# Two per-token rows through DRAM on ScalarE's queue, and all corrections on VectorE

## The chip, the cores and the metric

One core of one Trainium2 chip. The metric is the device time of one launch in microseconds (us), as the median of several runs; the span that a profile shows is about 1.8 us shorter. The runs that are compared ran on the same chip.

Engine names in the profile: PE is the matrix engine, DVE is VectorE, ACT is ScalarE, POOL is GpSimd, SP is the engine that here only issues transfers. ACTq and SPq are the instruction queues of ScalarE and SP when they issue a transfer. The prediction calls the transfers that SP and ScalarE issue HWDGE transfers. BU, in it, is the half-transformed data, which goes through DRAM and comes back in another order (the regrouping).

## The reference

```python
def reference(A_x, A_w_r, A_w_i, B_x, B_w_gate, B_w_up, B_w_down):
    x  = A_x                                   # (1, 2048, 640) bf16
    xn = _layernorm(x, axis=-1)                # eps 1e-5, no scale and shift
    s  = irfft2(rfft2(xn) * (w_r + 1j * w_i))  # over both axes
    g  = _silu((_gelu(xn @ w_gate) * (xn @ w_up)) @ w_down)   # 640 -> 1536 -> 640
    return x + s * g
```

Only the layer norm in front of `w_gate` and `w_up` matters here. For the first 512 tokens and the first two tiles of hidden features the kernel does not wait for the normalised input: it multiplies the raw `x`, and mends the product afterwards. With mean m and r = 1/sigma of a token, (x - m) r W = (x W + (-m) colsum(W)) r. The tokens lie along the free dimension of the product, so -m and r are needed as rows that stand on all 128 partitions. These rows are the subject of the change.

## The kernel before

The kernel is recorded as a list of tasks (`add`), each with the engines that may run it, an assumed duration, a rank and its inputs. A small simulator (`Plan.run`) then decides, before compilation, in which order each engine gets its instructions. A task's `land` is an assumed landing time, in ns, of a transfer; it overrides the simulator's own estimate. On the chip each engine works strictly in that order, so an instruction that waits holds all those behind it.

```python
# r and -m of 4 x 128 tokens lie as columns in RM; PE turns them into 8 rows, VectorE copies
# them out of PSUM, they go to DRAM (D5, 4 KB) and come back broadcast to 128 partitions (RB, 512 KB)
t  = add(rows_pe, "PE", ...)
t  = add(lambda e: nc.vector.tensor_copy(out=..., in_=sr.tile[0:8, 0, 0:P]), "DVE", ...)
rs = dma(D5, lambda: rt.tile[0:8, :], (0, -5, 0), 4096, after=[t], use=[rt])          # on SP
rb_in = dma(RB..., D5.rearrange("k t -> (k t)").partition_broadcast(P), (0, -5, 1), 524288, after=[rs])
...
def gate_up(grp, t):
    ...   # the matmuls of one tile of w_gate into pg and of w_up into pu (two PSUM buffers each)
    if not early:
        a = add(act, "ACT", ...)      # ge = gelu(pg)             -> frees pg
        u_done[grp, t] = add(mul, "DVE", ...)   # uT = pu * ge    -> frees pu
        return
    for k, (w, ps) in enumerate(((Wg, pg), (Wu, pu))):       # the two early tiles
        ...   # copy the raw product out of PSUM (IU for gate, R for up)
        m = add(... nc.vector.scalar_tensor_tensor(out=ev, in0=RB[:, 1], scalar=WSUM, in1=ev,
                                                   op0=mult, op1=add), "DVE", ..., after=[out, rb_in, ...])
        normed.append(add(... (nc.gpsimd if e == "POOL" else nc.vector).tensor_tensor(ev * RB[:, 0]),
                          "POOL" if k else "DVE", ..., after=[m]))
    ...   # then gelu and uT as above
...
with tc.manual_schedule():
    for t in plan.run():
        t.emit(t.on)
```

Beside these, ScalarE casts the folded halves of the Fourier transform out of PSUM (`mc<-sp`). Each cast frees a buffer that PE's next transform matmuls (`sp<-mb,F1T`) need.

## Time and profile before

| | before |
|---|---|
| time, median (lowest to highest) | 202.86 us (202.78 to 203.01) |
| span of the profiled run | 201.1 us |
| PE busy | 195.2 us, 97% |
| PE idle between 10 and 197 us | one hole of 0.38 us |
| RB, from issue to landing | 22.20 to about 29.7 us |

The prediction shows the views of this profile. Its lines read: start in us, duration, engine, source line, operation, output<-inputs, partitions x elements and type, count; in brackets the engine's idle time just before, and what ended it. These lines from the timelines of VectorE, GpSimd and PE (one fence each) are not among them:

```profile
29.71 0.75 DVE L920 SCALAR_TENSOR_TENSOR IU<-RB,WSUM,IU 128x512 f32<-128x512 f32 x1 [1.12 <-DMA RB<-D]
...
32.84 1.38 DVE L920 SCALAR_TENSOR_TENSOR IU<-RB,WSUM,IU 128x512 f32<-128x512 f32 x1
```

```profile
32.40 1.27 POOL L922 TENSOR_TENSOR R<-R,RB 128x512 f32<-128x512 f32 x1 [1.26 <-DVE R L920]
```

```profile
37.49 0.97 PE L970 MATMUL pg<-Wd,uT 128*128 128x320 bf16 x6 [0.38 <-ACT ge L903]
```

The first correction waits 1.12 us for RB; a correction beside GpSimd's multiply takes 1.38 instead of 0.75 us; and PE's only hole after 5.3 us is 0.38 us long.

### The profile page before, as it was taken

The page shows a single profiled execution, that of the slowest core. Times are in us where ns is not written, and L with a number is a line of the kernel's source. Part 1 is how long each engine was busy: PE and PEld are TensorE (multiplying, and loading weights), DVE is VectorE, ACT ScalarE, POOL GpSimd, SP SyncE. Part 2 cuts the span into 40 slices and gives each one's busy share as a digit, 9 for nine tenths or more (in the row PEclk, how much of TensorE's full clock was granted, in tenths as well). Part 3 has the DMA queues.
Part 4 walks back from the last instruction along what each step waited for, and adds up shares of the span by engine and source line. Part 5 has one row for each costly group of instructions (what it writes and reads, how often), then busy time and mean ns, then how long its engine had stood idle before and what let it go on. Part 6 is the DMA issues. An engine that isn't in the chain of part 4 may idle for free.

```text
span 201.1 us, 4125 instructions
## 1 busy us (share of the span) xinstructions
PE 195.2 (97%) x1527; PEld 117.4 (58%) x1527; DVE 149.7 (74%) x320; ACT 127.2 (63%) x224; POOL 33.1 (16%) x73
## 2 busy tenths in 40 slices
PE   7999999999999999999999999999999999999992
PEld 2994444566544555677755555467765555457781
DVE  3789969999323249999998999933257788887774
ACT  3898997974632768778775766333466565766421
POOL 2412347596000000000000000000004122211210
PEclk9999999999999999999999999999999999999999
DMA  6999999569949677333244210117704332332432
GB/s 175 329 316 325 344 392 235 126 165 196 301 128 375 223 202 178 103 93 115 61 126 126 75 50 16 68 49 221 317 3 135 96 132 100 98 107 92 130 103 65
DMA packets 35894, 32.62 MB, mean 162 GB/s; under 512 B 10910, under 2 KB 32930, under 8 KB 35874
## 3 DMA queue, kind: packets, MB, share of 16 engines
q1 hardware_dynamic: 34434, 29.49, 49.1%
q0 software_dynamic: 1152, 2.66, 4.8%
q10 hardware_dynamic: 288, 0.20, 0.5%
q8 instruction: 12, 0.20, 0.4%
q14 instruction: 8, 0.07, 0.1%
HBM read 22.51 MB, written 9.19 MB: 158 GB/s over the span
## 4 chain that ended last, share of the span: by engine, by line
PE 79%; DMA 10%; SPq 4%; DVE 3%; issue 1%; ACT 1%; DVEq 0%
PE pg L886 19%; PE pu L886 19%; PE pg L970 13%; PE pu L970 12%; DMA X<-in_A_x_dram 6%; SPq L303 4%; DMA RB<-D 4%; PE sp L697 3%; PE sp L830 3%; PE sp L772 2%; PE sp L806 2%; PE sp L670 2%; PE sp L532 1%; PE sp L690 1%; PE sp L824 1%
## 5 line engine op out<-in xcount | busy, mean ns | idle before, releaser
L886 PE MATMUL pu<-xnT,Wu 128*128 128x512 bf16 (+1 forms) x245 | 57.6, 366 | 0.0
L886 PE MATMUL pg<-xnT,Wg 128*128 128x512 bf16 (+1 forms) x245 | 57.5, 366 | 0.0
L907 DVE TENSOR_TENSOR uT<-pu,ge 128x512 bf16<-128x512 f32 x46 | 31.7, 689 | 20.9 <-PE pu L886 18.4
L970 PEld LDWEIGHTS <-uT 128*128 128x128 bf16 x396 | 37.8, 98 | 14.1 <-issue 0.6
L903 ACT ACTIVATE ge<-pg 128x512 bf16<-128x512 f32 x46 | 27.4, 597 | 25.5 <-PE pg L886 25.0
L886 PEld LDWEIGHTS <-Wg 128*128 128x128 bf16 x285 | 25.2, 98 | 22.1
L886 PEld LDWEIGHTS <-Wu 128*128 128x128 bf16 x285 | 25.1, 98 | 21.8
L970 PE MATMUL pg<-Wd,uT 128*128 128x320 bf16 (+2 forms) x204 | 30.5, 293 | 0.4 <-ACT ge L903 0.4
L970 PE MATMUL pu<-Wd,uT 128*128 128x320 bf16 (+1 forms) x192 | 29.7, 297 | 0.0
L296 ACT CAST ma<-sp 128x644 bf16<-128x644 f32 (+1 forms) x32 | 23.4, 792 | 9.7 <-PE sp L830 7.9
L932 POOL COPY xr<-s 1x1 bf16<-1x1 bf16 x1 | 0.2, 182 | 101.8 <-DVE s L856 101.8
L933 POOL DMA_DIRECT2D xr<-in_A_x_dram x16 | 8.8, 552 | 32.3 <-DVE res L957 31.7
L296 ACT CAST IU<-sp 128x640 bf16<-128x640 f32 x16 | 10.9, 691 | 4.2 <-PE sp L772 4.1
L979 ACT ACTIVATE th<-pg 128x320 f32<-128x320 f32 (+2 forms) x17 | 7.3, 427 | 9.9 <-PE pg L970 8.9
L296 ACT CAST Vt<-sp 128x640 bf16<-128x640 f32 x16 | 10.8, 691 | 3.7 <-PE sp L806 3.7
L984 DVE SCALAR_TENSOR_TENSOR G<-th,pg 128x320 bf16<-128x320 f32 (+1 forms) x16 | 7.7, 479 | 7.1 <-ACT th L979 6.9
L979 ACT ACTIVATE th<-pu 128x320 f32<-128x320 f32 (+1 forms) x16 | 7.0, 438 | 9.2 <-PE pu L970 9.0
L984 DVE SCALAR_TENSOR_TENSOR G<-th,pu 128x320 bf16<-128x320 f32 (+1 forms) x16 | 7.7, 480 | 5.6 <-ACT th L979 5.3
L296 ACT CAST mc<-sp 128x640 bf16<-128x640 f32 x15 | 9.8, 694 | 2.3 <-PE sp L533 1.3
L433 POOL TENSOR_TENSOR RSTD<-MVA,mh 128x1 f32<-128x1 f32 x12 | 8.4, 697 | 4.5 <-DVE MVA L415 3.7
L848 DVE TENSOR_TENSOR mb<-ma 128x640 bf16<-128x640 bf16 x8 | 3.9, 493 | 6.9 <-ACT ma L296 6.9
L750 DVE TENSOR_TENSOR R<-Y 64x644 bf16<-64x644 bf16 x16 | 7.8, 490 | 0.4
(107 smaller groups left out, 252.9 us busy)
## 6 DMA issues: line engine op xcount, KB each, us to landing
BU<-D SPq DMA_DIRECT2D x8, 640.0 KB
D<-mc SPq DMA_DIRECT2D x8, 320.0 KB
D<-IU SPq DMA_DIRECT2D x8, 320.0 KB
xr<-in_A_x_dram POOLq DMA_DIRECT2D x16, 160.0 KB, 2.6
out_dram<-res SPq DMA_DIRECT2D x15, 160.0 KB
Wg<-in_B_w_gate_dram SPq DMA_DIRECT2D x6, 320.0 KB
Wu<-in_B_w_up_dram SPq DMA_DIRECT2D x6, 320.0 KB
Wd<-in_B_w_down_dram SPq DMA_DIRECT2D x6, 320.0 KB
```

The source lines that it names most:

```text
L296: return nc.scalar.copy(out=out, in_=in_) if e == "ACT" else nc.vector.tensor_copy(out=out, in_=in_)
L303: return add(lambda e: nc.sync.dma_start(out=out() if callable(out) else out, in_=in_() if callable(in_) else in_), "SP", (430, 430), rank ...
L433: nc.gpsimd.tensor_tensor(out=rstd, in0=var, in1=mh, op=ALU.pow)
L697: nc.tensor.matmul(into(q, ri), lhsT=sZ.tile[:, q, ri, :], rhs=FM[:, kinds[q][2] + (4 if ri and kind == 0 else 0), :], start=False, stop=T ...
L750: nc.vector.tensor_tensor(out=o, in0=Yf[:, ::-3, :], in1=Yf[:, 1:3, :], op=ALU.subtract)
L886: nc.tensor.matmul(ps.tile[:, lo:hi + more], lhsT=w[:, c, t * P:(t + 1) * P], rhs=XR[:, c, lo + (lo > 0):hi + 1 if lo or more else hi] if ...
L903: nc.scalar.activation(out=ge.tile, in_=pg.tile if src is None else src, func=ACT.Gelu_apprx_tanh)
L907: nc.vector.tensor_tensor(out=u.tile, in0=pu.tile if src is None else src, in1=ge.tile, op=ALU.mult)
L933: nc.gpsimd.dma_start(out=sx.tile, in_=xv[:, n1, :])
L970: nc.tensor.matmul(ps.tile[:, 0:hi - lo], lhsT=uT[grp, ks[i]].tile[:, j * P:(j + 1) * P], rhs=Wd[:, ks[i], lo:hi], start=(i == 0), stop=(i ...
L979: nc.scalar.activation(out=th.tile[:, 0:hi - lo], in_=ps.tile[:, 0:hi - lo], func=ACT.Tanh, scale=0.5)
L984: nc.vector.scalar_tensor_tensor(out=G2.tile[:, lo:hi], in0=th.tile[:, 0:hi - lo], scalar=1.0, in1=ps.tile[:, 0:hi - lo], op0=ALU.add, op1 ...
```

## The change

The intent: RB waits on SP behind several microseconds of weight loads. On ScalarE's queue it should come earlier. The planner is told so (17.0 and 20.8 us), and places the corrections earlier. With the second multiply on VectorE too, no engine stands in the other's way.

```diff
-    rs = dma(D5, lambda: rt.tile[0:8, :], (0, -5, 0), 4096, after=[t], use=[rt])
-    rb_in = dma(RB.rearrange("p k n t -> p (k n t)"), D5.rearrange("k t -> (k t)").partition_broadcast(P), (0, -5, 1), 524288, after=[rs])
+    rs = add(lambda e: nc.scalar.dma_start(out=D5, in_=rt.tile[0:8, :]), "ACT", (600, 600), (0, -5, 0), after=[t], use=[rt], size=4096, land=17000)
+    rb_in = add(lambda e: nc.scalar.dma_start(out=RB.rearrange("p k n t -> p (k n t)"), in_=D5.rearrange("k t -> (k t)").partition_broadcast(P)),
+                "ACT", (600, 600), (0, -5, 1), after=[rs], size=524288, land=20800)
...
-            normed.append(add(lambda e, ev=ev: (nc.gpsimd if e == "POOL" else nc.vector).tensor_tensor(out=four(ev), in0=four(ev), in1=RB[:, 0], op=ALU.mult), *(("POOL", (1700, 1800), (1, 8)) if k else ("DVE", c_dve(512, 1), (0, 100))), after=[m], use=[ev]))
+            normed.append(add(lambda e, ev=ev: nc.vector.tensor_tensor(out=four(ev), in0=four(ev), in1=RB[:, 0], op=ALU.mult), "DVE", c_dve(512, 1), (0, 100), after=[m], use=[ev]))
```

## The prediction

> **What bounds the kernel now.** I read the page first, then the chain of waits, then the timelines of PE, ScalarE and the DMA-issuing SP queue from 10 to 40 us. The page's busy times and the chain's summary:
>
> ```profile
> PE 195.2 (97%) x1527; PEld 117.4 (58%) x1527; DVE 149.7 (74%) x320; ACT 127.2 (63%) x224; POOL 33.1 (16%) x73
> PE 79%; DMA 10%; SPq 4%; DVE 3%; issue 1%; ACT 1%; DVEq 0%
> ```
>
> PE is busy 195.2 of 201.1 us at full clock. The 5.9 us left are 1.21 at the start, 0.41 at 5.3 us, about 3.9 after the last matmul, and one hole of 0.38 at 37.1 us. So no change to VectorE, GpSimd or a transfer can win more than about 0.4 us unless it removes matmuls, and this one removes none. PE has no spare time after 5.3 us in which to win back a stall: whatever stops PE lengthens the run one for one.
>
> The chain passes through the transfers that the change moves:
>
> ```profile
> 4.39 5.97 DMA X<-in_A_x_dram
> 10.38 1.03 SPq L303
> ...
> 15.54 6.09 DMA X<-in_A_x_dram
> 21.64 0.52 SPq L303
> 22.20 7.48 DMA RB<-D
> 29.74 0.64 issue
> 30.38 0.68 DVE uT L907
> ```
>
> The reader should see two things. The broadcast RB takes 7.48 us from its issue, yet what it makes wait is small: in the wait view VectorE's first correction waited 1.1 us for it, and PE lost only the 0.38 us hole. And an issue on SP is released by the completion of a load issued six microseconds before (4.39 + 5.97 releases 10.38; 15.54 + 6.09 releases 21.64). The compiled instruction list explains it: HWDGE transfers take eight completion semaphores in turn, and each waits until the earlier user of its semaphore, eight transfers back, has landed. The SP timeline gives the landings:
>
> ```profile
> 10.38 1.03 SPq L303 DMA_DIRECT2D Wu<-in_B_w_up_dram  x1
> 11.45 1.49 SPq L303 DMA_DIRECT2D X<-in_A_x_dram  x2
> 12.99 1.24 SPq L303 DMA_DIRECT2D Wg<-in_B_w_gate_dram  x1
> 14.27 1.22 SPq L303 DMA_DIRECT2D Wu<-in_B_w_up_dram  x1
> ...
> 18.07 0.69 SPq L303 DMA_DIRECT2D Wu<-in_B_w_up_dram  x1
> ...
> 19.97 0.41 SPq L303 DMA_DIRECT2D D<-mc  x1
> 20.76 1.40 SPq L303 DMA_DIRECT2D Wd<-in_B_w_down_dram  x2
> ```
>
> The Wu load issued at 14.27 is the earlier user for the Wd load that starts at 20.76 after a 0.4 us wait, so it landed at 20.74. Between it and the first X load of 11.45 (tile 10) lie one X tile and two weight loads, 0.82 MB; at the 318 GB/s that the DMA view shows for 16 to 18 us that is 2.6 us, so X tile 10 landed at about 18.1. The issue at 18.07, which needed that semaphore, started without a visible wait: 18.05 us.
>
> ScalarE and PE at the moment where the change inserts the first transfer:
>
> ```profile
> 13.24 0.74 ACT L418 ACTIVATE th<-X 128x640 bf16<-128x640 bf16 x1
> 14.10 0.83 ACT L421 ACTIVATE th<-X,NM 128x640 bf16<-128x640 bf16 x1
> 14.93 1.18 ACT L903 ACTIVATE ge<-pg 128x512 bf16<-128x512 f32 x2
> 16.00 1.28 ACT L296 CAST mc<-sp 128x640 bf16<-128x640 f32 x2
> ```
>
> ```profile
> 15.85 1.24 PE L886 MATMUL pu<-xnT,Wu 128*128 128x512 bf16 x5
> 16.93 1.24 PE L886 MATMUL pg<-xnT,Wg 128*128 128x512 bf16 x5
> 18.01 0.38 PE L532 MATMUL sp<-mb,F1T 128*128 128x512 bf16 x1
> ```
>
> PE starts the pg group of 16.93 in the buffer that the first GELU (14.93) has emptied, and the transform of 18.01 in the buffer that the first cast (16.00) has emptied. Those two ScalarE instructions have about 1.4 us of slack, not more.
>
> **What the Trainium skill says.** "DMA: Bandwidth & Descriptors", section "Anatomy of one DMA", says that a semaphore wait belongs to the issuing sequencer, ahead of dispatch, and not to the DMA engines. The SP queue above behaves so; here it means ScalarE itself stands still. The same page, "Issuing engines are not separate DMA queues": issuing from another engine saves only sequencer time, the 16 engines are shared; the trace has them full (over 300 GB/s from 5 to 30 us), so the move adds no bandwidth. The same page, "Queues, rings and completion order": a DMA engine takes turns between queue rows by packets, so RB on ScalarE's row need not stand behind SP's backlog. No line of this trace shows that yet. "SBUF — State Buffer" calls the port pair of VectorE and GpSimd an exclusive lock. The trace agrees in tendency: the VectorE correction at 32.84 takes 1.38 us beside GpSimd's 1.27 us multiply at 32.40, and 0.75 us elsewhere; the uT multiply at 36.01 takes 1.16 instead of 0.67.
>
> **The change part by part.**
>
> 1. GpSimd loses two multiplies (1.27 and 1.36 us); VectorE gains two of about 0.68 us, 0.60 apart in the timeline: +1.2 us. The two slowed instructions give back 0.63 + 0.49 = 1.1 us. Net about zero, and it lies beside PE.
>
> 2. The move to D5 leaves SP (0.35 us) for ScalarE. In the compiled order it stands right after the mean pass that ends at 14.1 us and before the first GELU, and it waits for two semaphores: VectorE's copy (done 13.6 us) and the completion semaphore last used by X tile 10, which lands at 18.05. So ScalarE stops from 14.1 to 18.05: 4.0 us. The scheduler believed D5 would have landed by 17.0, and knows nothing of the semaphore. Issue 0.45 us (the X issue on ScalarE took 0.43): first GELU at 18.5, done at 19.1.
>
> 3. PE wanted that buffer at 16.93 and gets it at about 19.15: stall 2.2 us. It then wants the buffer of the first cast at 20.25. ScalarE after the GELU: variance pass 0.83, second GELU 0.50, cast 0.60, done at 21.0: stall 0.75 us.
>
> 4. RB follows on ScalarE at 21.0. It waits for D5 (issued 18.5, an estimate of 2.5 us by the page's fixed 2 us and some load, 21.0) and for the semaphore of the Wu load (20.74). ScalarE loses 0 to 0.5 us and 0.45 for the issue; the second cast ends at about 22.4, PE wants it at 22.4: 0.2 us. Sum so far 3.15 us.
>
> 5. RB lands about 4 us later, near 25.3: 2 us fixed by the page, and 0.52 MB at between half and all of 380 GB/s, 1.4 to 2.8 us (estimate). The new order has VectorE reach the first correction after the third uT multiply, near 23.8, so it stands for 1.5 us. The next uT multiply comes three corrections later (3 x 0.64 + 0.6 = 2.5 us), at 27.8; PE wants its pu buffer at about 28.3. No stall, unless RB lands after 25.8; I count 0.2 us.
>
> 6. The hole at 37.1 us (GELU of the last gate tile late) should go, since in the new order that GELU ends before PE wants its buffer: -0.38 us.
>
> 7. Later, SP issues five loads of the first spectral weights before the regrouping BU instead of after it, about 1.5 to 2.5 us later relative to PE. The first quarter of BU landed near 63.7 (an issue that needs its semaphore starts at 63.74) and is used at 65.83, so 2.1 us of slack: 0 to 0.4 us lost, counted 0.2.
>
> Sum: 2.2 + 0.75 + 0.2 + 0.2 - 0.38 + 0.2 = +3.2 us. Everything else shifts along with PE. 202.9 + 3.2 = 206.1 us, +1.6%.
>
> **The rivals.** (a) The intended effect: D5 lands at 17, RB at 20.8, corrections done by 27, the hole gone, 202.5 us. For it: RB indeed waits behind 6 us of backlog now, and a queue of its own takes turns. Against it: the hidden semaphore waits, and that there are only 0.4 us to win. (b) VectorE becomes the bound: from 15 to 25 us it is busy 9.6 of 10 us, and it now must do the corrections there while waiting in order for RB. If RB lands near 27, the uT multiplies release pu late and PE loses another 1.5 us: 207.5 to 208. For it: the lag of step 5 leaves only 0.5 us. Against it: ScalarE's stop has slowed PE and so given VectorE room. (c) The late start of BU costs 2 us more (208), if the weight loads hold the queue longer; against it, PE's own delay carries the whole chain along.
>
> **Range and chances.** Steps 2 to 4 depend on one landing known to about 0.3 us, on the issue time (0.4 to 1.1 us on SP under load) and D5's latency: about 1 us either way. Steps 5 and 7 add only upwards, up to 2 us. Range 204.4 to 207.8. The line of 2% is at 206.9: slower 0.28, within 0.70, faster 0.02, as the ceiling of gain is 0.4 us.
>
> **What would show it.** In the changed trace: ScalarE idle for about 4 us before the D5 issue, which starts near 18.1; the first GELU on pg near 18.5; PE idle about 2 us before the pg group that starts at 16.93 now, then some 0.7 us before the third transform; RB issued near 21 and landed near 25; the hole near 37 us gone; PE's busy sum unchanged. I am wrong if the D5 issue starts near 14 (the semaphore wait does not bind), if PE shows no hole between 16 and 23 us, or if PE's larger holes come at 28 us (rival b) or near 69 us (rival c).

## The result, and the profile after

| | before | after |
|---|---|---|
| time, median (lowest to highest, runs) | 202.85 us (202.78 to 203.01, 6) | 208.84 us (208.54 to 208.98, 6) |
| ratio of the mean times, 95% interval | | 1.0293 (1.0279 to 1.0306) |
| span of the profiled run | 201.1 us | 206.8 us |
| PE busy | 195.2 us | 196.4 us |
| mean granted clock | 1.00 | 0.989 |

A ratio here is the mean time of one kernel's fast runs over that of the other's in the same rounds, so it is not quite the ratio of the medians. The result is slower by 2.9%, 6.0 us, above the predicted range (204.4 to 207.8).

ScalarE's timeline of the kernel after (source lines from the change on are one higher than before):

```profile
18.45 0.53 ACTq L567 DMA_DIRECT2D D<-th  x1
19.02 0.60 ACT L904 ACTIVATE ge<-pg 128x512 bf16<-128x512 f32 x1 [4.99 <-DMA X<-in_A_x_dram]
...
20.80 0.69 ACT L296 CAST mc<-sp 128x640 bf16<-128x640 f32 x1
23.22 0.35 ACTq L568 DMA_DIRECT2D RB<-D  x1
23.61 0.69 ACT L296 CAST mc<-sp 128x640 bf16<-128x640 f32 x1 [2.12 <-DMA D<-th]
```

ScalarE stood twice. The first stop ends with the landing of an X tile that the first transfer does not read: the semaphore that it takes over. The second one waits for D5 itself: issued at 18.45, landed by 23.22, 4.8 us later. The cast of 23.61, whose input was ready, stood behind it.

VectorE's timeline of the kernel after:

```profile
24.83 0.69 DVE L908 TENSOR_TENSOR uT<-pu,ge 128x512 bf16<-128x512 f32 x1 [1.14 <-ACT ge L904]
28.00 0.75 DVE L921 SCALAR_TENSOR_TENSOR IU<-RB,WSUM,IU 128x512 f32<-128x512 f32 x1 [2.48 <-DMA RB<-D]
28.67 0.74 DVE L921 SCALAR_TENSOR_TENSOR R<-RB,WSUM,R 128x512 f32<-128x512 f32 x1
29.33 0.68 DVE L923 TENSOR_TENSOR IU<-IU,RB 128x512 f32<-128x512 f32 x1
29.93 0.68 DVE L908 TENSOR_TENSOR uT<-pu,ge 128x512 bf16<-128x512 f32 x1
```

RB landed at 28.00, only 1.7 us before its time on SP, and VectorE stood 2.48 us for it. In the new order three corrections stand ahead of the uT multiply of 29.93.

PE's timeline of the kernel after:

```profile
19.67 1.24 PE L887 MATMUL pg<-xnT,Wg 128*128 128x512 bf16 x5 [2.61 <-ACT ge L904]
21.54 0.58 PE L532 MATMUL sp<-mb,F1T 128*128 128x512 bf16 x1 [0.64 <-ACT mc L296]
...
22.03 2.34 PE L887 MATMUL pu<-xnT,Wu 128*128 128x512 bf16 x5
24.35 0.58 PE L532 MATMUL sp<-mb,F1T 128*128 128x512 bf16 x1
...
30.67 1.24 PE L887 MATMUL pu<-xnT,Wu 128*128 128x512 bf16 x5 [0.28 <-DVE uT L908]
...
43.04 0.39 PE L532 MATMUL sp<-mb,F1T 128*128 128x512 bf16 x1 [0.25 <-DVE mb L519]
```

The holes sum to 3.78 us. There is also the pu group of 22.03, which took 2.34 us instead of 1.24. The table by stretches of the same run shows why; after the busy times of PE, PEld, DVE, ACT and POOL its last three columns are the granted clock, the share of the DMA engines and GB/s:

```profile
18.00:20.00 2.00, 0.33 (x2) 0.19 (x2) 0.35 (x1) 0.98 (x2) 0.00 (x0) 1.00 1.14 337
20.00:22.00 2.00, 1.36 (x7) 0.47 (x5) 1.93 (x6) 1.49 (x4) 1.17 (x3) 0.85 1.12 332
22.00:24.00 2.00, 2.00 (x7) 0.77 (x6) 1.69 (x5) 0.39 (x1) 0.20 (x1) 0.50 1.13 324
```

PE ran at half clock behind its hole. And the DMA engines were full, 324 to 337 GB/s, while D5 was on its way.

The same work on PE starts later than before by these amounts: the first pg group after the stop by 2.74 us (16.93 to 19.67), the next by 5.19 (19.64 to 24.83), and from there it is 5.53 at the regrouped transform (65.83 to 71.36) and at the end of the last matmul (197.17 to 202.70). So the whole loss arises between 17 and 31 us, and 5.2 of it by 24.8 us.

### The profile page after: what moved, and what is told of

Same layout as the page of the kernel before. It is cut to its first block, busy times and chain, and to the rows that moved or that the text cites. A ratio compares the mean times of both kernels' runs of the same rounds, so it can differ in the third digit from the quotient of the medians.

```text
span 206.8 us, 4110 instructions
## 1 busy us (share of the span) xinstructions
PE 196.4 (95%) x1509; PEld 117.8 (57%) x1527; DVE 149.0 (72%) x321; ACT 126.9 (61%) x225; POOL 31.1 (15%) x71
## 4 chain that ended last, share of the span: by engine, by line
PE 80%; DVE 6%; DMA 6%; SPq 2%; issue 2%; ACT 1%; ACTq 0%; DVEq 0%
PE pu L887 21%; PE pg L887 19%; PE pg L971 12%; PE pu L971 12%; DMA X<-in_A_x_dram 6%; PE sp L698 3%; PE sp L831 3%; PE sp L773 2%; DVE uT L908 2%; SPq L303 2%; PE sp L807 2%; PE sp L532 2%; PE sp L671 2%; PE sp L691 1%; PE sp L825 1%
## 5 line engine op out<-in xcount | busy, mean ns | idle before, releaser
L887 PE MATMUL pg<-xnT,Wg 128*128 128x512 bf16 (+1 forms) x235 | 56.5, 365 | 3.1 <-ACT ge L904 2.6
L887 PE MATMUL pu<-xnT,Wu 128*128 128x512 bf16 (+1 forms) x237 | 58.3, 371 | 0.8 <-DVE uT L908 0.3
L887 PEld LDWEIGHTS <-Wu 128*128 128x128 bf16 x285 | 25.3, 98 | 22.8 <-issue 1.8
L296 ACT CAST mc<-sp 128x640 bf16<-128x640 f32 x16 | 10.8, 702 | 3.7 <-DMA D<-th 2.1
L433 POOL TENSOR_TENSOR RSTD<-MVA,mh 128x1 f32<-128x1 f32 x12 | 9.5, 797 | 1.0 <-DVE MVA L415 0.2
L418 ACT ACTIVATE th<-X 128x640 bf16<-128x640 bf16 x11 | 8.1, 739 | 0.0
```

Source lines behind the costliest of these rows:

```text
L296: return nc.scalar.copy(out=out, in_=in_) if e == "ACT" else nc.vector.tensor_copy(out=out, in_=in_)
L418: nc.scalar.activation(out=place(junk, (D,)), in_=x, func=ACT.Copy, scale=-1.0 / D, accum_out=less)
L433: nc.gpsimd.tensor_tensor(out=rstd, in0=var, in1=mh, op=ALU.pow)
L887: nc.tensor.matmul(ps.tile[:, lo:hi + more], lhsT=w[:, c, t * P:(t + 1) * P], rhs=XR[:, c, lo + (lo > 0):hi + 1 if lo or more else hi] if ...
```

## The experiments

Sixteen kernels, all with correct results, each beside the kernel before on the same chip. That kernel took 202.81 to 202.96 us in the median each time, so times of different rounds can be compared to about 0.2 us. (Beside run 16 one execution of the kernel before took 1155 us; it was left out as slow.)

| run | what is different | median us | ratio to before |
|---|---|---|---|
| 1 | before, all corrections on VectorE | 203.2 | 1.0017 |
| 2 | after, GpSimd keeps its multiplies | 209.61 | 1.0334 |
| 3 | after, issue and landing times told | 206.67 | 1.0187 |
| 4 | D5 and RB on GpSimd's queue, landings half told | 205.63 | 1.0128 |
| 5 | after, landings told | 207.3 | 1.0243 |
| 6 | GpSimd's queue, landings told | 202.7 | 0.9994 |
| 7 | after, D5's semaphore free earlier | 209.23 | 1.0326 |
| 8 | after, D5's semaphore free later | 211.26 | 1.0428 |
| 9 | after, RB issue and corrections moved back by hand | 210.42 | 1.0362 |
| 10 | GpSimd's queue, landings as in after | 208.87 | 1.0299 |
| 11 | after, PE's hole filled | 208.8 | 1.0293 |
| 12 | after, corrections moved back by hand | 209.05 | 1.0306 |
| 13 | after, later landings told, same end | 207.52 | 1.0245 |
| 14 | 13 with the semaphore earlier | 205.83 | 1.0152 |
| 15 | 13 with the semaphore later | 210.41 | 1.0379 |
| 16 | 13 with PE's hole filled | 207.04 | 1.0203 |

My theory after the result: the semaphore stop of ScalarE, then D5's slow landing, cost the time. The rivals: VectorE, which waits in order for RB; the half clock; the corrections on VectorE themselves.

### Runs 1 and 2: the two parts of the change alone

Run 1 is the kernel before with only the last line of the diff; run 2 is the kernel after without it.

> Half of the change: all corrections on VectorE, both transfers still on the SP queue. My theory (the loss comes from ScalarE standing still for completion semaphores that other transfers used before): within 0.3% of before, 202.4 to 203.4 us, no PE hole over 0.5 us. Rival (VectorE, with 1.2 us more of work in its busiest stretch, became the bound): at least 204.5 us.

> The other half: both transfers on ScalarE's queue, GpSimd keeps its two multiplies. My theory: as slow as the changed kernel, 208.0 to 209.5 us, with ScalarE idle near 5 us before the first transfer's issue at about 18.4 us and the PE clock at half for about 3 us after the hole. Rival (VectorE's extra work): near 203 to 204 us.

Run 1: 203.2 us, ratio interval 0.9991 to 1.0043; its profile has one hole of 0.64 us, near 49.5 us, where at most 0.5 was expected. Run 2: 209.61 us (209.44 to 209.93). So the multiplies cost nothing where they are, and the whole loss is that of the queue; beside it the move of the multiplies even helps (208.84 against 209.61). PE's holes of run 2:

```profile
23.81 0.38 PE L532 MATMUL sp<-mb,F1T 128*128 128x512 bf16 x1 [0.70 <-ACT mc L296]
...
30.73 1.24 PE L887 MATMUL pu<-xnT,Wu 128*128 128x512 bf16 x5 [1.10 <-DVE uT L908]
```

One thing I had expected was missing: after a first hole of 2.51 us the clock stayed full here. In place of the half clock PE waited, for the cast behind D5 (0.70 us) and for the uT multiply behind RB (1.10 us). That was the first sign that several limits lie on top of each other.

### Runs 3 and 4: tell the planner, or take another queue

```diff
 # run 3
+        at = max(at, getattr(t, "not_before", 0))     # in the planner
-..., "ACT", (600, 600), (0, -5, 0), after=[t], use=[rt], size=4096, land=17000)
+..., "ACT", (600, 600), (0, -5, 0), after=[t], use=[rt], size=4096, land=23200);  rs.not_before = 18500
-                "ACT", (600, 600), (0, -5, 1), after=[rs], size=524288, land=20800)
+                "ACT", (600, 600), (0, -5, 1), after=[rs], size=524288, land=28000);  rb_in.not_before = 23300
 # run 4
-    rs = add(lambda e: nc.scalar.dma_start(...), "ACT", ..., land=17000)
+    rs = add(lambda e: nc.gpsimd.dma_start(...), "POOL", ..., land=18500)
-    rb_in = add(lambda e: nc.scalar.dma_start(...), "ACT", ..., land=20800)
+    rb_in = add(lambda e: nc.gpsimd.dma_start(...), "POOL", ..., land=24000)
```

> The changed kernel, with its scheduler told what the trace measured: first transfer not before 18.5 us and landing at 23.2, broadcast not before 23.3 and landing at 28.0. Both stay on ScalarE's queue, only later in its order, behind work that is ready. My theory: ScalarE no longer stands still (under 0.7 us before each issue), PE has no hole over 0.5 us, 202.5 to 203.6 us, although the broadcast lands as late as in the changed kernel, near 28 us. Rival (ScalarE's queue itself is slow or harmful, whenever it is used): stays above 206 us.

> The changed kernel with both transfers issued by GpSimd, whose transfers take their semaphores from a separate set that nothing else uses at this time. My theory: the first transfer is issued near 14.5 us at once, as no foreign landing has to be awaited; ScalarE and PE run as before, 202.5 to 204 us. GpSimd may stand a few us for the landing of the first transfer, which delays some 1/sigma results. Rival (the 16 engines are full and any early broadcast takes bandwidth that PE needs): PE holes waiting for weights, above 205 us.

Both missed: 206.67 and 205.63 us. In run 3 the later place in the list gave both transfers other semaphores. RB's was one that a Wd load had used, and ScalarE stood 3.65 us for that load:

```profile
26.41 0.60 ACT L907 ACTIVATE ge<-pg 128x512 bf16<-128x512 f32 x1 [3.65 <-DMA Wd<-in_B_w_down_dram]
```

That stop left PE a hole of only 0.35 us. PE's largest hole came later: RB landed at 32.36 us, VectorE stood 2.52 us for it, and PE behind VectorE:

```profile
35.03 2.29 PE L890 MATMUL pu<-xnT,Wu 128*128 128x512 bf16 x5 [2.25 <-DVE uT L911]
```

So an order told to the planner moves the semaphores too, and run 3 doesn't test its theory. In run 4 GpSimd, whose semaphores nobody had used, issued D5 at 14.04 at once, and ScalarE never stood. But D5 landed 5.9 us later and RB another 8.4 us later, and now VectorE stood (its timeline, then PE's):

```profile
28.41 0.75 DVE L921 SCALAR_TENSOR_TENSOR IU<-RB,WSUM,IU 128x512 f32<-128x512 f32 x1 [4.24 <-DMA RB<-D]
```

```profile
29.82 1.24 PE L887 MATMUL pu<-xnT,Wu 128*128 128x512 bf16 x5 [1.81 <-DVE uT L908]
```

RB, issued right behind D5, came at 28.0 us from ScalarE's queue and at 28.4 from GpSimd's. From here on I held two causes: ScalarE stands (for the semaphore, then for D5), and VectorE stands for RB, because the plan puts the corrections at a landing that the full DMA engines don't give.

### Runs 5 and 6: the landings told, on either queue

```diff
 # run 5: the kernel after, D5 and its semaphore stay where they are
-..., size=4096, land=17000)            +..., size=4096, land=23200)
-..., size=524288, land=20800)          +..., size=524288, land=28000)
 # run 6: run 4 with
-..., size=4096, land=18500)            +..., size=4096, land=20000)
-..., size=524288, land=24000)          +..., size=524288, land=28500)
```

> The changed kernel, but its scheduler is told when D5 and RB really land (23.2 and 28.0 us in place of 17.0 and 20.8). In the instruction list D5 keeps its place on ScalarE and keeps X tile 10's completion semaphore; the RB issue moves behind the casts, and VectorE's corrections move behind the uT multiplies. Theory of two causes (ScalarE stands for the semaphore; VectorE stands in order for RB): the first stays whole, ScalarE idle from 14 to about 18.4 us and PE's hole of about 2.6 us near 17 to 19.7, the second goes (VectorE waits under 0.5 us for RB, no PE hole from uT near 30 us): 205.2 to 206.2 us. Rival, that the semaphore stop explains all 6 us of loss: 208.3 to 209. Rival, that the wait for RB explains all: under 204.

> The fourth experiment's kernel (D5 and RB issued by GpSimd, whose semaphores nobody else has used yet), but its scheduler is told the landings that that run showed (20.0 and 28.5 us). Theory of two causes: both are gone now, ScalarE and PE run as in the kernel before and VectorE waits for RB under 0.5 us; 202.4 to 203.6 us, PE holes under 0.8 us in sum between 10 and 45 us. Rival, that the corrections on VectorE or the transfers on another queue cost something of their own that these two do not cover: 204.5 us or more, with a PE hole near 30 to 42 us that a uT multiply ends.

Run 6 hit: 202.7 us, interval of the ratio 0.9978 to 1.0009, and PE has no hole at all after 1.2 us in its profile. With neither engine standing for D5 or RB, all of the loss is gone. It is also the best version here, and it equals the kernel before; a gain of the size of the 0.38 us hole would not be told from noise here.

Run 5 gave 207.3 us, against 205.2 to 206.2 expected. None of PE's holes (1.70, 0.64, 0.16 us) comes from a uT multiply, as expected; VectorE still waited 0.84 us for RB, which landed at 32.26 (expected: under 0.5). The first hole is shorter than the expected 2.6 us because PE came to it late: the pu group that starts at 15.85 before started at 16.60, since matmuls between 4.3 and 7 us had taken longer. It ends at 19.54, as in the kernel after. The last matmul ended at 200.14, 2.97 us after that of before. But the re-planned order had left more to do behind it, 5.5 us to the end against 3.9. That is a by-product of the planner, so runs 13 to 16 came back to it.

### Runs 7 and 8: move the semaphore

The number of transfers ahead of D5 decides whose semaphore it takes over. Run 7 joins loads ahead of it; run 8 adds five tiny ones.

```diff
 # run 7
-    load_x(10, 11)
-    load_x(11, 12)
+    load_x(10, 12)
-    load_x(12, 14)
-    load_x(14, 16)
+    load_x(12, 16)
 # run 8, in the loop that emits the tasks
+            if t is x_in[12]:
+                for k in range(5):
+                    nc.sync.dma_start(out=tiny[:, k, :], in_=tabs["f1"][0:16, 16 * k:16 * k + 16])
```

> The changed kernel with the loads of X tiles 10 and 11 joined into one and those of 12 to 15 into one, same bytes and same order on every computing engine. D5 then takes the completion semaphore of an earlier weight load (the first Wg load behind X tile 9), which should land near 16.6 us and not 18.4. Semaphore theory: D5 starts at 16.5 to 17.2, the first GELU follows 0.6 us later, PE's first hole shrinks from 2.6 to 0.8 to 1.5 us, and the time falls by 0.8 to 1.8 us against the changed kernel: 207.0 to 208.0. Rival (the issue on ScalarE itself, or D5's own data, is what stops ScalarE): the D5 issue stays at 18.4 and the time at 208.5 to 209.

> The changed kernel with five loads of 16x16 numbers (0.5 KB each, never used) on SP just behind X tile 12's load: same order on every computing engine, but D5 takes the completion semaphore of a weight load further on, which should land near 19.5 to 20 us. Semaphore theory: D5 starts at 19.5 to 20.2 and not at 18.45, ScalarE's idle time and PE's first hole grow by 1.1 to 1.7 us, and so does the time: 209.9 to 210.6. Rival: the semaphore is not what ScalarE waits for, D5 stays at 18.4 and the time at 208.5 to 209.2.

The semaphore did what it should in both: D5 started at 16.66 and at 20.24 (18.45 in the kernel after), each time behind another load. Timelines of ScalarE, VectorE and PE in run 7:

```profile
16.66 0.53 ACTq L565 DMA_DIRECT2D D<-th  x1
17.23 0.60 ACT L902 ACTIVATE ge<-pg 128x512 bf16<-128x512 f32 x1 [2.77 <-DMA Wg<-in_B_w_gate_dram]
```

```profile
27.86 0.75 DVE L919 SCALAR_TENSOR_TENSOR IU<-RB,WSUM,IU 128x512 f32<-128x512 f32 x1 [3.73 <-DMA RB<-D]
```

```profile
17.88 1.24 PE L885 MATMUL pg<-xnT,Wg 128*128 128x512 bf16 x5 [0.39 <-ACT ge L902]
...
22.96 0.38 PE L530 MATMUL sp<-mb,F1T 128*128 128x512 bf16 x1 [1.69 <-ACT mc L296]
...
30.54 1.24 PE L885 MATMUL pu<-xnT,Wu 128*128 128x512 bf16 x5 [1.75 <-DVE uT L906]
```

PE's first hole shrank from 2.61 to 0.39 us, and the time did not fall: 209.23 us. The 2.2 us came back as longer waits for the cast behind D5 (1.69) and for RB (1.75), which landed at 27.86, 0.14 us earlier than before. The expected gain of 0.8 to 1.8 us is missed, and the reason is in these lines. Run 8 lost 2.4 us (211.26 us, against 209.9 to 210.6 expected); RB landed at 30.08.

Run 8 also measured D5's latency on idle DMA engines by accident, in the row of its table by stretches in which D5 was under way:

```profile
20.00:22.00 2.00, 0.54 (x2) 0.26 (x2) 0.56 (x1) 1.19 (x2) 0.00 (x0) 0.54 0.09 23
```

The loads on SP stood too, the DMA engines moved only 23 GB/s, and D5, issued at 20.24, had landed when RB's issue, which waits for it, started at 22.34: at most 2.1 us. With the engines full the same 4 KB took 4.1 to 5.2 us from ScalarE's queue (runs 2, 7, 9, 11, 12 and the kernel after) and 5.9 to 6.1 us from GpSimd's (runs 4, 6, 10). That is the number which the prediction had at 2.5.

The kernels of the table below have this VectorE order and the change's multiplies, and show one rule (run 2, whose second multiplies are on GpSimd, has the same 2.67 us to the pu group):

| | RB landed | pu group behind the corrections | last matmul ended | less RB's landing |
|---|---|---|---|---|
| after | 28.00 | 30.67 | 202.70 | 174.70 |
| run 7 | 27.86 | 30.54 | 202.57 | 174.71 |
| run 8 | 30.08 | 32.75 | 204.78 | 174.70 |
| run 11 | 28.29 | 30.96 | 203.04 | 174.75 |
| run 10 | 27.51 | 30.18 | 203.26 | 175.75 |

The pu group starts 2.67 us after RB's landing: three corrections, one uT multiply and nothing else. From there PE runs without a further stop worth naming. (Run 10 ended about another microsecond later; its clock was lower, below.)

### Runs 9 and 12: corrections moved back by hand

Run 12 reorders the finished list: the corrections and what depends on them come behind the next two uT multiplies. Run 9 does so behind three, and puts RB's issue on ScalarE behind the next two casts and the GELU between them.

```diff
+    todo = plan.run()
+    # run 9 only: RB's issue three ScalarE tasks later
+    todo.remove(rb_in); todo.insert(place_of, rb_in)
...
+    # tasks between the first correction and the n-th next uT multiply (n = 2 or 3):
+    # those that need RB, directly or through a buffer, go to the end of the stretch
...
+    todo[first:uts + 1] = kept + late
```

> The changed kernel with two pieces moved and nothing re-planned: RB's issue stands on ScalarE behind the next two casts and the GELU between them, so that no ready cast waits for D5's landing; and VectorE's corrections stand behind the next three uT multiplies, so that none waits behind RB. The same PE order. Left of the loss are the semaphore stop and what follows it directly (steps 2 and 3 of the prediction). Theory: ScalarE still idle until 18.4 us, PE holes of about 2.6 and 0.6 us and then no more than 0.2 to 0.5, 205.6 to 206.5 us. Rival, that the 6 us come from the semaphore stop alone: 208.3 to 209. Rival, that they come from RB alone: below 204.

> The changed kernel with VectorE's corrections behind the next two uT multiplies, RB's issue left where it is. PE's hole of 0.28 us before the pu group of 30.67 goes. Theory: ScalarE's two waits had by then delayed PE as far as RB would have, so that only 0.2 to 0.5 us come back: 208.2 to 208.8 us. Rival, that RB alone holds the time in the changed kernel: 205.5 to 207.

Run 12: 209.05 us (208.69 to 209.47), no gain, and just above the range. VectorE no longer waited for RB, but PE still had 2.54, 0.63 and 0.87 us of holes for ScalarE, and two new ones (0.34 and 0.63 us near 33 to 35 us) where corrections in a row now held later buffers. So RB's wait taken away in this way won nothing; but the two new holes cost about 1 us, so a gain of that size may hide behind them. Run 9 missed clearly: 210.42 us. Its first half went well: holes of 1.84 and 0.64 us, then none until 34 us, and PE reached the pg group of 24.83 (kernel after) at 23.05. Then my reordering made a wait of its own: a GELU of corrected data came ahead of ready GELUs on ScalarE. ScalarE's timeline of run 9, then PE's:

```profile
34.91 0.63 ACT L904 ACTIVATE ge<-IU 128x512 bf16<-128x512 f32 x1 [1.84 <-DVE IU L923]
```

```profile
36.79 1.52 PE L887 MATMUL pg<-xnT,Wg 128*128 128x512 bf16 x5 [2.79 <-ACT ge L904]
```

So the run's total tests nothing, though its first half bears on step 4 (below). Eight corrections and multiplies of 0.6 us each need to be spread between the uT multiplies, and the planner does that better than my hand.

### Run 10: RB's wait alone

The transfers on GpSimd's queue as in run 4, but with the planned landings of the kernel after, so that VectorE meets the corrections as early as there.

> The reverse of the ninth: D5 and RB issued by GpSimd, so that ScalarE never stands, but with the planned landings (17.0 and 20.8 us) of the changed kernel, so that VectorE meets the corrections as early as there. In four kernels so far that have this VectorE order, the pu group that starts behind the first corrections started 2.67 us after RB's landing, and the last matmul ended 174.7 us after it. If RB lands near 28.4 as it did on this queue: no PE hole before 26 us, then holes of 4 to 6 us in sum that a uT multiply ends, the pu group near 31.1, last matmul near 203.1, 208.6 to 209.8 us. So ScalarE's stop taken away would win nothing. Rival, that ScalarE's stop is the cause: 203 to 205.8 us.

208.87 us: a hit. ScalarE never stood for D5 or RB; PE ran without a hole until 26 us, as in the kernel before; and then it lost everything at one place. The timelines of VectorE and of PE:

```profile
27.51 0.75 DVE L921 SCALAR_TENSOR_TENSOR IU<-RB,WSUM,IU 128x512 f32<-128x512 f32 x1 [3.85 <-DMA RB<-D]
```

```profile
30.18 1.51 PE L887 MATMUL pu<-xnT,Wu 128*128 128x512 bf16 x5 [4.14 <-DVE uT L908]
```

The time is that of the kernel after (208.84) though both of ScalarE's stops are gone. A hole of 4.14 us and about 1.7 us at a lower clock behind it (this group and the next two start 1.30, 2.13 and 1.49 us before their successors instead of 1.08) make the same loss. ScalarE stood for RB too, though it didn't issue it: 6.34 us before a GELU of corrected data, until VectorE had corrected it.

### Run 11: the half clock

```diff
+                    for _ in range(2 if grp == 0 and t == 3 and w is Wu else 0):
+                        for c in range(5):
+                            nc.tensor.matmul(...)   # the same group, overwritten by the real one
```

> The changed kernel with two more repeats of one pu group on PE (2.16 us of matmuls whose result is the same and overwritten) just ahead of the 2.6 us hole. It fills the hole, so that PE should not run at half clock from 21.5 to 24.6 us. If the half clock costs time of its own: 207.3 to 208.0 us. If the second cast (done 24.3 us) and RB (28.0 us) would hold PE there anyway: the half clock goes, holes of 0.6 to 1.2 us before a fold and before the pu group of 30.7 us come in its place, and the time stays at 208.3 to 209.1.

208.8 us, with a clock of 1.00 in the stretch: a hit. Without the half clock the kernel after is no faster: other waits take its place. PE's holes that stand in its place:

```profile
23.82 0.38 PE L532 MATMUL sp<-mb,F1T 128*128 128x512 bf16 x1 [0.61 <-ACT mc L296]
...
30.96 1.24 PE L891 MATMUL pu<-xnT,Wu 128*128 128x512 bf16 x5 [1.31 <-DVE uT L912]
```

### Runs 13 to 16: the semaphore stop with nothing behind it

The kernel after, with 23.2 and 32.0 us told. That puts RB's issue behind the casts and the corrections behind RB's landing in this order (VectorE never waits for RB), and leaves the end of the kernel as it is in the kernel after. Runs 14, 15 and 16 add the edits of runs 7, 8 and 11 to it.

> As the fifth run, but told 32.0 us for RB, the landing that the fifth run showed, which also gives the changed kernel's order of work at the end. Left are steps 2 and 3. Theory: D5 issued near 18.4 us, PE holes of 2.4 to 3.4 us in sum between 10 and 45 us, VectorE waits under 0.3 us for RB, 3.7 to 4.2 us from the last matmul's end to the end: 205.3 to 206.4 us. Rival, that the tail of the fifth run was no accident: 207 us or more.

> The thirteenth with the joined X loads of the seventh (D5's semaphore free near 16.7 us). If the semaphore's landing sets the time once RB is out of the way: PE's first hole 0.2 to 0.6 us, holes 0.8 to 1.6 us in sum, 203.4 to 204.7 us, at least 1 us below the thirteenth. If the order of the casts or RB still bounds it as in the seventh: within 0.5 us of the thirteenth.

> The thirteenth with the five small loads of the eighth (D5's semaphore free near 20.2 us). Theory: PE's first hole 3.9 to 4.5 us, after it some 3 us at half clock as in the eighth (nothing waits there now, so that it costs up to 1.5 us), 207.0 to 209.0 us, at least 1.3 us above the thirteenth.

> The thirteenth with the eleventh's two repeats of a pu group ahead of PE's hole (2.16 us of matmuls, result unchanged). The hole is filled to about 0.6 us and the clock stays full. If the half clock costs its 1.5 to 1.8 us here: 205.4 to 206.3 us, which is what steps 2 and 3 of the prediction add up to. If not: 207.0 us or more.

PE's first hole in runs 14, 13 and 15, in this order, one fence each:

```profile
17.74 1.24 PE L885 MATMUL pg<-xnT,Wg 128*128 128x512 bf16 x5 [0.32 <-ACT ge L902]
```

```profile
19.85 1.24 PE L887 MATMUL pg<-xnT,Wg 128*128 128x512 bf16 x5 [2.78 <-ACT ge L904]
```

```profile
21.50 2.29 PE L887 MATMUL pg<-xnT,Wg 128*128 128x512 bf16 x5 [4.45 <-DMA D<-th]
```

(Run 15's hole is put down to D5's landing; the GELU that PE needs, which stood behind D5's issue, also ended just then, at 21.45.) 205.83, 207.52 and 210.41 us: with RB out of the way, the semaphore's landing (D5 starts at 16.52, 18.63, 20.28 us) is worth its time, which it was not in run 7. All three lie about 1 us or more above what I expected. One part of that shows in the profile: a hole of 0.93 us near 42 to 45 us in each, where a transform matmul (`sp<-mb`) waits for VectorE, which is now busy with the late corrections. Run 13 falls on the side of its rival (207 us or more), but not for the rival's reason: it ends 3.96 us after its last matmul, as expected.

Run 16 took the half clock away and gave 207.04 us, not 205.4 to 206.3, so the half clock was not what held run 13 above its range. The filler (the two repeated groups) took 2.2 us of PE where run 13 has its hole, then follow holes of 0.64, 0.16 and 0.93 us. The last matmul ended 4.05 us late (201.22 against 197.17). The starts of PE's groups divide this better than the holes do, since the profile lets groups that start 1.08 us apart last 1.24 us, and so shows a hole up to 0.16 us too short. PE was 0.20 us late before the stop (16.05 against 15.85), and 3.68 us behind it (the pg group of 19.64 started at 23.32). So the stop by itself cost 3.5 us, and the new order with its late corrections the remaining 0.4 us. The half clock is worth 1.6 us between the two profiled runs and 0.5 us between the medians. The profiled execution of run 13 was its slowest by 1 us, at the same mean clock as the other three (0.988 to 0.992); why is not shown.

## Why the prediction was wrong, point by point

The chance of a slower kernel was put at 0.28, the time 2.7 us too low.

- **Step 1, the multiplies: right.** Run 1 shows 203.2 us, no change; VectorE's corrections all take 0.74 or 0.75 us there, none of them slowed by a GpSimd multiply.
- **Step 2, the semaphore stop: right.** D5 started at 18.45 us (predicted 18.05) after the landing of X tile 10, and runs 7 and 8 moved it with the semaphore, to 16.66 and 20.24.
- **Step 3, what follows on PE: right.** Holes of 2.61 and 0.64 us, predicted 2.2 and 0.75. With nothing behind it, the stop cost 3.5 us (run 16), 0.5 more than these two terms.
- **Step 4, RB's issue behind D5: this step failed.** "An estimate of 2.5 us" for D5's landing was 4.8. The second cast, counted to end at 22.4 us, ended at 24.30, and PE lost about 1.9 us there instead of 0.2: the next pg group is 5.19 us late, of which 2.61 + 0.64 are step 3. In the trace of the kernel after this loss looks like half clock; runs 2, 7, 11 and 12, at full clock, show a wait for the cast in that place (0.70, 1.69, 0.61 and 0.87 us). Runs 5 and 9, where RB's issue stands behind these two casts, reach that pg group at 23.36 and 23.05 us and not at 24.83: 1.5 to 1.8 us of the loss is gone there. I had read that the DMA engines were full, and yet took a latency that run 8 shows only for nearly idle engines. (The page's table with the fixed 2 us is, besides, one for GpSimd's path, and D5 went by ScalarE's.)
- **Step 5, RB: same error, and hidden by step 4.** RB landed at 28.0, not 25.3: 2.2 us of that because it was issued at 23.22 and not at 21.0, 0.5 because it took 4.8 us. The prediction's own rule, "No stall, unless RB lands after 25.8", held: 28.0 - 25.8 would be 2.2 us of stall. It shows as 0.28 us only, because step 4 had already taken as much; that this is close to the 0.2 us counted is luck. Run 10 shows RB alone making the whole loss.
- **Step 6, the old hole: right.** It went. Another of 0.25 us at 43 us came.
- **Step 7, the regrouping: 0 instead of 0.2.** PE is 5.53 us late before it (51.26 to 56.79) and behind it (65.83 to 71.36).

The sum of the measured steps is 2.61 + 0.64 + 1.94 + 0.28 - 0.38 + 0.25 = 5.34 us, against 5.53 at the last matmul. By its own signs the prediction had the path right: PE's two larger holes came between 17 and 21.6 us, and not at 28 or 69. But it expected PE's busy sum unchanged, and this rose from 195.2 to 196.4 us, with the half clock that it didn't foresee. Rival (b) was the right one to fear, and named the right place, but its argument against ("ScalarE's stop has slowed PE and so given VectorE room") holds only for an early RB.

What the experiments add is that these costs are not a sum of which each part could be had back. Taking away RB's wait (run 12, at the price of two new holes), the half clock (run 11), most of the first stop (run 7) or both of ScalarE's stops (run 10) left 208.8 to 209.2 us each time. Only with ScalarE's and VectorE's waits both gone (run 6) did the time return. A list of holes in one trace doesn't tell this.

The intent failed on its first premise: a queue of its own did not bring RB much earlier (28.0 against 29.7 us). RB itself took 4.8 us there and not 7.5, but it was issued 1.0 us later (23.22 against 22.20), because D5 came late. The Trainium skill says that transfers run on the same 16 DMA engines whichever engine issues them ("DMA: Bandwidth & Descriptors", section "Issuing engines are not separate DMA queues"), and this case agrees: RB landed at 27.5 to 28.4 us from GpSimd's queue, issued at 20.0 to 20.6, and at 27.9 to 28.3 from ScalarE's, issued at 21.8 to 23.2 (the kernel after and runs 2, 7, 11).

Open: why PE is up to 0.75 us late before the stop in some executions, and what the half clock costs by itself. That a hole sets off the half clock was seen, not explained.

## What to carry to other kernels

Before a transfer moves to a computing engine, look up which earlier transfer it shares a completion semaphore with, and what ready work stands behind its issue: the engine stands until that other transfer has landed. A consumer in a strict order must be placed at a landing measured under the load of that moment, not at that of an idle system: on GpSimd's queue the same two transfers cost 6 us with the landings that were hoped for (run 10), and nothing with measured ones (run 6). And when several waits end at nearly the same time, take them away together as well as one by one, since each alone may give nothing back.

## What the Trainium skill lacked or had wrong

- "DMA: Bandwidth & Descriptors", section "Anatomy of one DMA — SWDGE (gpsimd) path", gives, for GpSimd's path, a fixed part of about 2.0 us per transfer that scales with nothing. For a transfer of 4 KB the runs show 5.9 to 6.1 us on that path at 300 GB/s and more of other traffic (runs 4, 6, 10); on ScalarE's they show 4.1 to 5.2 us at such traffic and at most 2.1 us at 23 GB/s (run 8). The page's later row on HBM latency under load (section "Latency and other measured facts") points in this direction; the fixed figure should name the load.
- No page that I found says that transfers of SP and ScalarE take eight completion semaphores in turn, so that an issue waits for the transfer eight before it, though unrelated (counted in the full SP timeline of the kernel before: the load issued at 15.54 releases the issue of 21.64, and runs 7 and 8 move D5's by changing the count): 4.99 us of idle ScalarE in the kernel after, 2.77 us and 6.33 us with the semaphore moved (runs 7 and 8).
- "TensorE: Matmul & The Clock Gate", part 1, names an idle window of about 3.4 us, free-running, for the fall to half clock. Here holes of 2.25 us (run 3), 2.61 us (kernel after) and 2.78 us (run 13) were followed by some 3 us at half clock, while holes of 2.51 us (run 2) and 2.54 us (run 12) were not. Shorter holes than the figure can suffice, and the length of the hole alone does not decide.
